# Attention, gated layer and rational layer on one core: when block 0 transposes, when the first pair is split, and in what order weights are streamed

## The chip, the cores and the metric

The kernel runs on one core of a Trainium2 chip. The metric is the device time of one execution in microseconds (us). A core has TensorE (PE in the profile, its weight loads PEld), VectorE (DVE), ScalarE (ACT), GpSimd (POOL) and SyncE (SP), which here issues nearly all DMA transfers. Each engine works off its own instructions in the order in which the program emits them and waits on semaphores for the others.

## The reference

All numbers are float32. There are 8 batches with 8 heads, 576 positions and head size 64; keys and values are averaged over 8 positions, so 72 of them remain.

```
k_p, v_p = mean over 8 positions of k, v
attn     = softmax(q @ k_p^T / 8) @ v_p             # -> x: 4608 tokens x 512
x        = (silu(x @ w_gate) * (x @ w_val)) @ w_out # 512 -> 1536 -> 512
h        = x @ w_in                                 # 512 -> 2048
out      = (a0 + a1 h + a2 h^2 + a3 h^3) / (1 + |b0||h| + |b1| h^2 + 1e-6) @ w_out2
```

## The kernel before, in words

The 4608 tokens are cut into nine blocks of 512. Each large product is made of three fp32r matmuls of 128x512 per tile: high times high, low times high and high times low part. `split` makes the parts: ACT copies a tile into fp32r (L97), DVE (L94) or POOL (L101) subtracts that from the source.

**Block 0** (L784 to L821) runs the gated layer plainly in 12 steps f = 0 to 11. A step emits for TensorE: the gate product gp (12 matmuls), the value product vp (12), and the output product acc of step f - 1 (12, `out_mm`). In each step `first.step(6)` runs three times; it carries the conversion of the weights one stage on (words and rounding on ACT, shifts, selects and low parts on DVE, an addition on POOL). Between these stands the attention of blocks 1 and 2, the first pair, in units of 128 or 64 rows. `attention_slots` puts the pieces of unit n into named places of the steps, and `place` emits them: scores (PE, tile sc) at the end of step n in place "C"; in step n + 1 `soft1` on DVE in place "0" (maximum L380 and subtraction L383, once for each of two score banks), the exponential on ACT in "A" (L393), and sums, division (POOL, L408) and copies in "B2"; in step n + 2 the transposes `t_` (PE, tile t) and, when a group of one or two units is complete, the products with the values `v_` (PE, tile pv). ACT moves the transposes out (L440, L441), DVE takes a low part (`evac_low`, L445), and ACT copies pv into xraw (L470). At a change of batch `v_` also calls `build_vs` (POOL L322, L330, then ACT L336). Units 0 to 8 have 64, 128, 128, 128, 64, 128, 128, 128, 128 rows; the groups are units 0; 1 and 2; 3 and 4; 5; 6 and 7; 8.

Scores, transposes and value products of block 0 take their PSUM banks from one pool of two:

```python
    ps_at = ctx.enter_context(tc.tile_pool(name="ps_at", bufs=2, space=PSUM))
    def bank(name, i=None):
        pool, tag = (ps_at, "at") if i is None else ...
```

One unit's scores take both banks, so do its transposes, and a group's value products take both as two halves (two head pairs in each).

**Pairs** (L886 to L962): the eight other blocks go in four pairs p through a seven-product scheme over 2x2 parts (n = 12 p + f, 48 steps). In a step TensorE has seven products of six matmuls: s1 t1, s2 t2, a22 t4 of step n - 1, a12 b21, s4 b22, a11 b11 of step n + 1, s3 t3. `token_sums` makes t1 to t4 by subtraction (L737), `token_part` splits tokens, `sum_weights` and `sum_splits` make s1 to s4 in the first pair, `sum_store` stores them, and `stream` loads them back for the other three pairs. In the same steps `second` (class `Halves`) converts the weights of the last layer: `begin` stores the finished half (L204), loads raw halves (L199) and starts conversion; of the buffers that it uses at first there are three. Then `hidden` outputs go to DRAM (L855) and q, k and v of the next blocks are loaded (L276). All these transfers stand in SP's one queue, in program order. The output product follows (L1022 to L1087; PSUM tiles ya, yb, yc), and then the rational layer (L1128 on).

Of the kernel before, what the change touches and what calls it, by code (L numbers as in the profile page):

```python
# [10 lines left out]
F32 = mybir.dt.float32  # L11
# [3 lines left out]
ALU = mybir.AluOpType  # L15
# [4 lines left out]
P = 128  # L20
B, H, S, D = 8, 8, 576, 64
# [43 lines left out]
def attention_gated_rational(  # L65
# [13 lines left out]
    def wslot(name, shape=(P, 2, 512), dt=F32R):  # L79
        return wp.tile(list(shape), dt, tag="w", name=name)  # L80

    def f32(ap):
        return ap.bitcast(F32)
# [402 lines left out]
    def attention_slots(js, start, helped=False, heads=False):  # L486


        def put(slot, place, fn):
            plan.setdefault((slot, place), []).append(fn)  # L490

        groups = [g for j in js for g in units(j)]
        owner = [j for j in js for g in units(j)]
        box = {}
        fl = [(g, i) for g in range(len(groups)) for i in range(len(groups[g]))]

        def do_xraw(j):
            if (j - PLAIN) % 2:
                live["w"] += 2
                st["xraw", j] = [wslot(f"xraw{j}_{i}", (P, 2, BLK), F32) for i in range(2)]  # L500
            else:
                t = keep.tile([P, KT, BLK], F32, tag="xraw", name=f"xraw{j}")
                st["xraw", j] = [t[:, 0:2, :], t[:, 2:4, :]]
        for n, (g, i) in enumerate(fl):
            u = groups[g][i]
            slot = start + n
            put(slot - 1, "B2", lambda u=u: box.__setitem__(("q", u), qload(u)))
            put(slot, "C", lambda u=u: box.__setitem__(("s", u), scores(u, box.pop(("q", u)), False, helped, heads)))
            put(slot + 1, "A0" if slot + 1 >= PLAIN * NF1 else "0", lambda u=u: box["s", u][0]())
            put(slot + 1, "0" if heads else "A", lambda u=u: box["s", u][1]())  # L510
            put(slot + 1, "B" if slot + 1 >= PLAIN * NF1 else "B2", lambda u=u: [fn() for fn in box.pop(("s", u))[2:]])

            def t_(u=u, g=g, i=i, at_bank=0 if slot + 2 >= PLAIN * NF1 else None):
                if i == 0:
                    box["pt", g] = new_pt(f"{js[0]}_{g}")
                for fn in transposes(u, box["pt", g], i * P, at_bank):
                    fn()
            put(slot + 2, "A", t_)
            if i + 1 == len(groups[g]):
                def v_(g=g):  # L520
                    j = owner[g]
                    if ("xraw", j) not in st:
                        do_xraw(j)
                    values(groups[g], box.pop(("pt", g)), st["xraw", j])
                    if g + 1 < len(groups) and groups[g + 1][0][0] != groups[g][0][0]:
                        build_vs(groups[g + 1][0][0])
                put(slot + 2, "B", v_)


    jobs = prep_jobs(0, early=True)  # L530
# [102 lines left out]
    def sum_weights(f):  # L633

        if f >= NF1:
            return
        rg, rv = sums_w[f] = [ldp.tile([P, 2, QUART], F32, tag="ld", name=f"r{x}{f}") for x in "gv"]
        for r, w in zip((rg, rv), (W1[f"g{f}"], W1[f"v{f}"])):
            nc.vector.tensor_tensor(r.rearrange("p h c -> p (h c)"), f32(w[:, 0, :]), f32(w[:, 1, :]), op=ALU.add)
        (a11, a12), (a21, a22) = ([r[:, h] for h in range(2)] for r in (rg, rv))  # L640
        nc.gpsimd.tensor_tensor(a22, a21, a22, op=ALU.add)
        nc.gpsimd.tensor_tensor(a21, a11, a21, op=ALU.subtract)
        nc.gpsimd.tensor_tensor(a11, a22, a11, op=ALU.subtract)
        nc.gpsimd.tensor_tensor(a12, a12, a11, op=ALU.subtract)

    def sum_splits(f):
        if f >= NF1:
            return
        rg, rv = sums_w.pop(f)
        w = [wslot(f"ws{f}_{i}") for i in range(2)]  # L650
        for i, r in enumerate((rv, rg)):
            split(w[i][:, 0, :], w[i][:, 1, :], r.rearrange("p h c -> p (h c)"))
        g_w, v_w = W1.pop(f"g{f}"), W1.pop(f"v{f}")
        streamed[f] = {
            "a11": (g_w, 0), "a12": (g_w, 1), "s3": (w[0], 0), "s1": (w[0], 1),
            "s2": (w[1], 0), "s4": (w[1], 1), "a22": (v_w, 1),
        }

    def sum_store(f):
        if f >= NF1:  # L660
            return
        x = streamed[f]
        for i, key in enumerate(("s1", "s2")):
            nc.sync.dma_start(s_d[f][i], f32(x[key][0]))
        if f < RESIDENT:
            nc.sync.dma_start(w_d[f], f32(x["a11"][0]))
            nc.sync.dma_start(v_d[f][:, :, QUART:], f32(x["a22"][0][:, :, QUART:]))
# [56 lines left out]
    def place(stage, f, p_):  # L724
        for fn in plan.pop((stage * NF1 + f, p_), []):
            fn()


    sums_x, parts_x = {}, {}

    def token_sums(p, eng):
        (b11, b21), (b12, b22) = (st.pop(("xraw", j)) for j in PAIRS[p])
        t1, t2, t3, t4 = (wslot(f"t{p}_{i}", (P, 2, BLK), F32) for i in range(4))

        def sub(out, x, y, eng=eng):
            for i in range(2):
                eng.tensor_tensor(out[:, i, :], x[:, i, :], y[:, i, :], op=ALU.subtract)  # L737
        sub(t1, b12, b11)
        sub(t2, b22, t1)
        sub(t3, b22, b12, nc.gpsimd)  # L740
        sub(t4, b21, t2, nc.gpsimd)
        sums_x[p] = {"b11": b11, "b21": b21, "b22": b22, "t1": t1, "t2": t2, "t3": t3, "t4": t4}
        parts_x[p] = {}

    FIRST_HOMES = {"b22": (0, 1), "t4": (2, 3)}

# [6 lines left out]
        for i in range(2):  # L753
            split(tiles[i][:, 0, :], tiles[i][:, 1, :], src[:, i, :])

    def stream(n):
        if NF1 <= n < len(PAIRS) * NF1:
            f = n % NF1
            w = [wslot(f"sw{n}_{i}") for i in range(4)]
            for t, src in zip(w, (s_d[f][0], w_d[f], s_d[f][1])):  # L760
                nc.sync.dma_start(f32(t), src)
            nc.sync.dma_start(f32(w[3][:, :, :QUART]), v_d[f][:, :, QUART:])
            streamed[n] = {
                "a11": (w[1], 0), "a12": (w[1], 1), "s3": (w[0], 0), "s1": (w[0], 1),
                "s2": (w[2], 0), "s4": (w[2], 1), "a22": (w[3], 0),
            }

    def part_product(acc, n, weights, tokens, first):
        w, c = streamed[n][weights]
# [7 lines left out]
    def out_mm(f):  # L777
        ht, w = h_t.pop(f), W1.pop(f"o{f}")
        for i in range(KT):
            mm3(acc[i], [(w, slice(i * P, (i + 1) * P), ht, full)], first=f == 0, last=f == NF1 - 1)  # L780
        live["w"] -= 1

    place(0, -1, "B2")
    for f in range(NF1):  # L784
# [30 lines left out]
        if f:  # L815
            out_mm(f - 1)
        place(0, f, "C")
        if f == NF1 - 2:
            sum_weights(0)
        if f == NF1 - 1:  # L820
            token_sums(0, nc.vector)  # L821
    first.finish()
    second.load()
    token_part(0, "b11")
    token_part(0, "t1")
    out_mm(NF1 - 1)
    ys = [wslot(f"ys_{i}", (P, 2, BLK), F32) for i in range(2)]
    for i in range(KT):
        nc.scalar.activation(ys[i // 2][:, i % 2, :], acc[i], AF.Copy)
# [49 lines left out]

        return 2 if n % 2 and n > NF1 + 2 else int(n > 0)  # L880

    sum_store(0)
    sum_weights(1)
    begin_chain(0)
    token_part(0, "t2")
    for n in range(full_n):  # L886
        p, f = divmod(n, NF1)
        stage = PLAIN + p
# [14 lines left out]
            second.paired = True  # L903
        second.begin(turns(n), turns(n + 1))
        part_product(bank_a[n], n, "s2", "t2", False)
        nc.vector.tensor_tensor(c, cq[n][:, 0, :], bank_a[n], op=ALU.add)  # L906
        if f == 0:
            if n == 0:
                token_part(p, "b21")
            token_part(p, "b22")  # L910
        place(stage, f, "A0")
        place(stage, f, "A")
# [4 lines left out]
            token_part(p + 1, "t2")  # L917
        second.middle()
        sum_splits(n + 1)
        stream(n + 2)  # L920
        b = bank_b.pop(n)
        part_product(b, n, "a12", "b21", False)
        if f == 0:
            token_part(p, "t3")
        hq[n] = wslot(f"hq{n}", (P, 2, BLK), F32)
# [7 lines left out]
        if n > 0:  # L933
            keep_hidden(n - 1)
        second.end()
        sum_store(n + 1)
        reload(n + 4)
        sum_weights(n + 2)
        if 0 < p < 3:
# [4 lines left out]
                (out_store if i else out_parts)(3 * p - 4 + r)  # L944
        place(stage, f, "B2")
        part_product(bank_a[n], n, "s3", "t3", False)
        nc.vector.tensor_tensor(cq[n][:, 1, :], cq[n][:, 0, :], bank_a[n], op=ALU.add)  # L947
        if f == 0:
            token_part(p, "t4")
# [3 lines left out]
        if p + 1 == len(PAIRS):  # L953
            if f == NF1 // 2 + 1:
                out_weights("a11")
                for k in range(5):
                    left_load(0, k)
            if f == NF1 - 2:
                left_load(0, 5)
                out_weights("s1")  # L960
            if f == NF1 - 1:
                out_weights("s2")  # L962
    NK = NF1 // 2
    TOKENS = ("b11", "t1", "t2", "b21", "t3", "b22", "t4")
# [56 lines left out]
    nc.scalar.preload_act_table_set("natural_log_exp_and_others")  # L1021
    for p, (j1, j2) in enumerate(PAIRS):  # L1022
        final = p + 1 == len(PAIRS)
        pool, tag = ((ps_gv, "gv"), (ps_at, "at"))[p % 2]
        ba = [pool.tile([P, BLK], F32, tag=tag, name=f"ya{p}_{q}") for q in range(2)]
        bb, bc = {}, {}
        box = {}
# [206 lines left out]
```

## Time and profile before

| what | us |
|---|---|
| three runs | 1772.21, 1769.96, 1768.76; median 1769.96 |
| profiled execution | 1774.04, of which the span shown is 1772.2 |
| PE busy | 1720.2 (97%), weight loads 1408.5 (79%) |
| DVE busy | 1425.7 (80%) |
| ACT busy | 1161.4 (66%) |
| POOL busy | 326.1 (18%) |
| mean granted TensorE clock | 0.993 of 2.4 GHz |

Busy time is the sum of an engine's instructions over the span. Block 0 lies between 36 and 182 us, the four pairs up to 755 us, the output product up to 985 us and the rational layer behind it.

### The profile page before, as it was taken

What the parts mean: (1) busy time and instruction counts of PE and PEld (TensorE: products, weight loads), DVE (VectorE), ACT (ScalarE), POOL (GpSimd) and SP (SyncE); (2) the same over time, 40 slices, a digit from 0 to 9 for tenths busy, and PEclk for the clock granted to TensorE, in tenths of its full rate; (3) what the DMA queues carried; (4) which work ended last, traced back from release to release, by engine and by line L of the source; (5) the groups of instructions that cost most, each with busy time, mean ns of one, the idle gap of its engine ahead of it and who ended that gap; (6) DMA issues with size and microseconds to landing.
All of it is one profiled execution on the core that took longest, in us unless ns stands there. A gap on an engine that the chain in (4) does not pass through costs nothing.

```text
span 1772.2 us, 23731 instructions
## 1 busy us (share of the span) xinstructions
PE 1720.2 (97%) x8104; PEld 1408.5 (79%) x8104; DVE 1425.7 (80%) x2325; ACT 1161.4 (66%) x2044; POOL 326.1 (18%) x412
## 2 busy tenths in 40 slices
PE   6898899999999999999999999999999999999999
PEld 5677677778878878778888788888888888888887
DVE  7998987777677664387778799989898989898987
ACT  5897766467577654455554677776777777777775
POOL 3455554534634431200000000000000000000000
PEclk9999999999999999999999999999999999999999
DMA  7775587899999899995517500000000000000000
GB/s 279 266 275 218 214 309 260 288 342 356 373 323 333 330 324 334 359 397 214 190 60 261 202 20 29 24 25 24 24 24 25 24 25 24 25 24 25 0 25 24
DMA packets 131736, 305.72 MB, mean 173 GB/s; under 512 B 12960, under 2 KB 53024, under 8 KB 130592
## 3 DMA queue, kind: packets, MB, share of 16 engines
q1 hardware_dynamic: 130752, 303.61, 47.4%
q8 instruction: 64, 1.05, 0.2%
q10 hardware_dynamic: 864, 0.60, 0.1%
q14 instruction: 56, 0.46, 0.1%
HBM read 207.16 MB, written 96.99 MB: 172 GB/s over the span
## 4 chain that ended last, share of the span: by engine, by line
PE 79%; DVE 8%; DMA 5%; ACT 3%; POOL 2%; issue 2%; SPq 1%; POOLq 0%; DVEq 0%; ACTq 0%
PE h L260 22%; PE acco L260 22%; PE ca L260 11%; PE ya L1077 6%; PE cc L260 6%; PE yc L1077 3%; PE cb L260 2%; PE yb L1077 2%; PE sc L372 1%; PE pv L461 1%; DMA q<-in_q 1%; POOL t L737 1%; DMA sw<-wd 1%; PE t L433 1%; DVE kr L291 1%
## 5 line engine op out<-in xcount | busy, mean ns | idle before, releaser
L260 PE MATMUL h<-z,wi 128*128 128x512 f32 x1728 | 414.7, 389 | 2.2 <-ACT yq L1046 2.2
L260 PE MATMUL acco<-wo,gt 128*128 128x512 f32 x1728 | 414.6, 389 | 0.0
L260 PEld LDWEIGHTS h<-z,wi 128*128 128x128 f32 x1728 | 324.2, 188 | 69.8 <-ACT yq L1046 2.6
L260 PEld LDWEIGHTS acco<-wo,gt 128*128 128x128 f32 x1728 | 324.4, 188 | 67.4
L1143 ACT ACTIVATE sq<-h 128x512 f32<-128x512 f32 x144 | 85.8, 596 | 176.0 <-PE h L260 176.0
L1150 DVE SCALAR_TENSOR_TENSOR w<-sq,neg,w 128x512 f32<-128x512 f32 x144 | 107.9, 750 | 43.8 <-ACT w L1144 43.7
L1164 ACT ACTIVATE gt<-g 128x512 fp32r<-128x512 f32 x144 | 90.9, 631 | 32.8 <-DVE g L1160 32.8
L1160 DVE SCALAR_TENSOR_TENSOR g<-t,neg,e 128x512 f32<-128x512 f32 x144 | 108.3, 752 | 5.1
L1156 DVE SCALAR_TENSOR_TENSOR t<-t,neg,h 128x512 f32<-128x512 f32 x144 | 107.7, 748 | 5.1
L1147 ACT ACTIVATE t<-h,neg 128x512 f32<-128x512 f32 x144 | 111.7, 776 | 0.0
L1157 DVE SCALAR_TENSOR_TENSOR e<-w,ln 128x512 f32<-128x512 f32 x144 | 98.6, 685 | 13.5 <-ACT ln L1154 13.5
L1154 ACT ACTIVATE ln<-ln,lnb 128x512 f32<-128x512 f32 x144 | 104.3, 724 | 4.7
L1144 ACT ACTIVATE w<-h,cab 128x512 f32<-128x512 f32 x144 | 98.6, 685 | 8.2 <-DVE e L1157 8.1
L1158 DVE SCALAR_TENSOR_TENSOR e<-e,ln 128x512 f32<-128x512 f32 x144 | 99.7, 692 | 5.0
L906 DVE TENSOR_TENSOR cc<-cq,ca 128x512 f32<-128x512 f32 x48 | 33.3, 693 | 84.0 <-PE ca L260 84.0
L1165 DVE TENSOR_TENSOR gt<-g,gt 128x512 fp32r<-128x512 f32 x144 | 99.0, 687 | 2.2 <-ACT gt L1164 0.8
L1155 DVE TENSOR_TENSOR t<-t,h 128x512 f32<-128x512 f32 x144 | 98.4, 683 | 0.0
L1153 ACT ACTIVATE ln<-w 128x512 f32<-128x512 f32 x144 | 91.5, 635 | 0.2 <-DVE w L1150 0.2
L901 ACT ACTIVATE cq<-cc 128x512 f32<-128x512 f32 x48 | 28.6, 596 | 86.6 <-PE cc L260 86.6
L947 DVE TENSOR_TENSOR cq<-cq,ca 128x512 f32<-128x512 f32 x48 | 32.5, 678 | 54.5 <-PE ca L260 54.5
L124 POOL TENSOR_TENSOR rawo<-rawo 128x256 uint32<-128x256 uint32 (+1 forms) x44 | 37.6, 855 | 147.8 <-DVE rawo L121 62.6
L408 POOL TENSOR_TENSOR p<-p,sm 128x576 f32<-128x576 f32 (+1 forms) x40 | 52.3, 1308 | 62.2 <-DVE sm L407 43.9
(276 smaller groups left out, 3455.1 us busy)
## 6 DMA issues: line engine op xcount, KB each, us to landing
sw<-sd SPq DMA_DIRECT2D x72, 512.0 KB, 6.8
h<-hq SPq DMA_DIRECT2D x48, 512.0 KB, 7.3
sw<-wd SPq DMA_DIRECT2D x36, 512.0 KB, 6.7
sd<-ws SPq DMA_DIRECT2D x24, 512.0 KB, 5.3
hl<-h SPq DMA_DIRECT2D x24, 512.0 KB, 6.5
hr<-h SPq DMA_DIRECT2D x24, 512.0 KB, 10.0
sw<-vd SPq DMA_DIRECT2D x36, 256.0 KB, 7.3
out<-ob SPq DMA_DIRECT2D x36, 256.0 KB, 2.2
```

Of the source, the lines that this page charges most:

```text
L260: nc.tensor.matmul(acc, st[:, lw, cols], mv[:, rw, mcols], start=first and i == 0, stop=last and i == n - 1, skip_group_check=seeded,)
L1077: nc.tensor.matmul(banks[q], w[:, lw, cols], t[:, rw, :], start=opened and k == 0 and m == 0, stop=k == NK - 1 and m == 2, skip_group_chec ...
L1144: nc.scalar.activation(w0, hps, AF.Abs, scale=cab[:, 4:5])
L1147: nc.scalar.activation(t, hps, AF.Identity, scale=neg[:, 3:4], bias=neg[:, 2:3])
L1150: nc.vector.scalar_tensor_tensor(w0, sq, neg[:, 5:6], w0, op0=ALU.mult, op1=ALU.add)
L1154: nc.scalar.activation(ln, ln, AF.Exp, scale=-1.0, bias=lnb)
L1155: nc.vector.tensor_tensor(t, t, hps, op=ALU.mult)
L1156: nc.vector.scalar_tensor_tensor(t, t, neg[:, 1:2], hps, op0=ALU.add, op1=ALU.mult)
L1157: nc.vector.scalar_tensor_tensor(e, w0, C1, ln, op0=ALU.add, op1=ALU.mult)
L1158: nc.vector.scalar_tensor_tensor(e, e, 2.0, ln, op0=ALU.subtract, op1=ALU.mult)
L1160: nc.vector.scalar_tensor_tensor(g, t, neg[:, 0:1], e, op0=ALU.add, op1=ALU.mult)
L1165: lambda gt=gt, g=g: nc.vector.tensor_tensor(gt[:, 1, :], g, f32(gt[:, 0, :]), op=ALU.subtract),
```

## The change

In block 0 the transposes move from place "A" (behind gp) to "B" (behind vp), and the value products from "B" to a new place "D" behind the scores. Of the first pair's sums, t1 and t2 and the split of b11 move to the end of step 10, the split of t2 ahead of the pairs; t3 and t4 move into step n = 0, on POOL. s1 and s2 now share one tile, s3 and s4 the other, by another order of the four POOL operations. `stream` loads single pieces, each behind the product that used that piece's predecessor. `sum_store` runs one step later, and the load of a raw half ahead of the pairs (`second.load()`) goes. Loads of `left_load` are spread over steps, and the two PSUM pools of ya swap.

```diff
-            put(slot + 2, "A", t_)
+            early = slot + 2 < PLAIN * NF1
+            put(slot + 2, "B" if early else "A", t_)
...
-                put(slot + 2, "B", v_)
+                put(slot + 2, "D" if early else "B", v_)
...
-        nc.gpsimd.tensor_tensor(a22, a21, a22, op=ALU.add)
-        nc.gpsimd.tensor_tensor(a21, a11, a21, op=ALU.subtract)
-        nc.gpsimd.tensor_tensor(a11, a22, a11, op=ALU.subtract)
-        nc.gpsimd.tensor_tensor(a12, a12, a11, op=ALU.subtract)
+        nc.gpsimd.tensor_tensor(a11, a11, a21, op=ALU.subtract)
+        nc.gpsimd.tensor_tensor(a21, a21, a22, op=ALU.add)
+        nc.gpsimd.tensor_tensor(a22, a22, a11, op=ALU.subtract)
+        nc.gpsimd.tensor_tensor(a12, a12, a22, op=ALU.subtract)
...
-    def stream(n):
+    def stream(n, *pieces):
         if NF1 <= n < len(PAIRS) * NF1:
...
+            for i in pieces:
+                w = wslot(f"sw{n}_{i}")
+                if i == 3:
+                    nc.sync.dma_start(f32(w[:, :, :QUART]), v_d[f][:, :, QUART:])
+                else:
+                    nc.sync.dma_start(f32(w), (w_d[f], s_d[f][0], s_d[f][1])[i])
...
         place(0, f, "C")
+        place(0, f, "D")
         if f == NF1 - 2:
             sum_weights(0)
-        if f == NF1 - 1:
-            token_sums(0, nc.vector)
+            token_sums(0, nc.vector, ("t1", "t2"))
+            token_part(0, "b11")
     first.finish()
-    second.load()
-    token_part(0, "b11")
     token_part(0, "t1")
     out_mm(NF1 - 1)
+    token_part(0, "t2")
...
-    sum_store(0)
     sum_weights(1)
     begin_chain(0)
-    token_part(0, "t2")
...
         part_product(bank_a[n], n, "s2", "t2", False)
+        stream(n + 2, 1)
...
                 token_part(p, "b21")
+                token_sums(0, nc.gpsimd, ("t3", "t4"))
             token_part(p, "b22")
...
         sum_splits(n + 1)
-        stream(n + 2)
+        stream(n + 1, 3)
         b = bank_b.pop(n)
         part_product(b, n, "a12", "b21", False)
+        stream(n + 2, 0)
...
-        sum_store(n + 1)
+        sum_store(n)
...
         part_product(bank_a[n], n, "s3", "t3", False)
+        stream(n + 2, 2)
...
-                for k in range(5):
-                    left_load(0, k)
+            if f >= NF1 // 2 + 2:
+                left_load(0, f - NF1 // 2 - 2)
...
-        pool, tag = ((ps_gv, "gv"), (ps_at, "at"))[p % 2]
+        pool, tag = ((ps_at, "at"), (ps_gv, "gv"))[p % 2]
```

## Rows read from the trace of the kernel before

**Rows 1.** Busy time by stretch; columns as named in the first line.
```profile
core 0: us, PE busy (x) PEld busy (x) DVE busy (x) ACT busy (x) POOL busy (x), PEclk, DMA share, GB/s
53.80:166.05 112.25, 103.78 (x564) 83.15 (x563) 104.56 (x196) 97.21 (x158) 53.23 (x60) 0.97 0.71 254
198.50:345.00 146.50, 137.27 (x700) 110.23 (x700) 117.41 (x201) 88.70 (x160) 84.08 (x102) 0.96 0.79 278
984.90:1772.20 787.30, 783.65 (x3456) 648.58 (x3456) 705.64 (x1041) 560.12 (x933) 0.00 (x0) 1.00 0.08 30
```

**Rows 2.** Waits of DVE, 50 to 166 us: total, times, longest.
```profile
DVE ptr L445 <- ACT ptr L440: 4.1, 9, 1.2
```

**Rows 3.** Timeline of PE, steps 4 and 5: start, length, instruction [idle before].
```profile
89.25 0.60 PE L461 MATMUL pv<-pt,vs 128*128 128x256 f32 x2
...
91.46 2.92 PE L260 MATMUL acc<-ht,wo 128*128 128x512 f32 x12
...
94.97 3.06 PE L260 MATMUL gp<-x,wg 128*128 128x512 f32 x12
97.86 0.60 PE L433 MATMUL t<-ident,p 128*128 128x128 f32 x4
```

**Rows 4.** Timeline of DVE in step 5.
```profile
96.63 0.45 DVE L383 TENSOR_TENSOR p<-sc,mx 64x288 f32<-64x288 f32 x1
...
97.47 0.45 DVE L383 TENSOR_TENSOR p<-sc,mx 64x288 f32<-64x288 f32 x1
...
100.04 0.42 DVE L445 TENSOR_TENSOR ptr<-t,ptr 32x256 fp32r<-32x256 f32 x1 [0.39 <-ACT ptr L440]
...
104.25 0.69 DVE L803 TENSOR_TENSOR hh<-hh,vp 128x512 f32<-128x512 f32 x1
```

**Rows 5.** Timeline of ACT, steps 4 and 5.
```profile
92.25 1.06 ACT L470 ACTIVATE xraw<-pv 128x512 f32<-128x512 f32 x2
...
96.04 0.67 ACT L155 ACTIVATE wo<-rawo 128x512 fp32r<-128x512 f32 x1 [0.51 <-POOL rawo L124]
...
97.85 1.28 ACT L794 ACT_TABLE_LOAD   x1
...
99.64 0.37 ACT L440 ACTIVATE ptr<-t 96x256 fp32r<-96x256 f32 x1
...
100.51 1.28 ACT L393 ACT_TABLE_LOAD   x1
...
102.40 0.67 ACT L155 ACTIVATE wg<-rawg 128x512 fp32r<-128x512 f32 x1
```

**Rows 6.** Timeline of POOL, then ACT, where `build_vs` runs.
```profile
127.13 1.49 POOL L322 TENSOR_TENSOR vs<-vp,vmask 128x512 f32<-128x512 f32 x1
...
129.40 0.42 ACT L336 ACTIVATE vr<-vt 96x256 fp32r<-96x256 f32 x1 [1.09 <-POOL vt L330]
```

**Rows 7.** Timeline of PE: what follows its longer waits.
```profile
59.78 0.69 PE L433 MATMUL t<-ident,p 64*128 64x64 f32 x4 [2.84 <-POOL p L408]
...
60.67 5.40 PE L260 MATMUL vp<-x,wv 128*128 128x512 f32 x12
...
249.99 1.12 PE L372 MATMUL sc<-kr,q 64*128 64x72 f32 x16 [1.11 <-DMA q<-in_q]
...
267.31 1.98 PE L372 MATMUL sc<-kr,q 64*128 64x72 f32 x16 [4.34 <-DMA q<-in_q]
269.22 2.93 PE L260 MATMUL cc<-x0t,ws 128*128 128x512 f32 x6
```

**Rows 8.** Timeline of PE at the start of the pairs.
```profile
184.18 0.50 PE L260 MATMUL ca<-x0b,wg 128*128 128x512 f32 x1 [0.50 <-DVE x0b L94]
...
188.34 0.49 PE L260 MATMUL ca<-x0t,ws 128*128 128x512 f32 x1 [0.65 <-DVE x0t L94]
```

**Rows 9.** Waits of SP's queue, 178 to 345 us.
```profile
SPq L199 <- DMA i_parts<-rawi: 33.1, 6, 6.7
```

**Rows 10.** Timeline of PE late in pair 4, and where the rational layer starts.
```profile
729.73 1.63 PE L260 MATMUL ca<-x3b,sw 128*128 128x512 f32 x6 [2.25 <-DMA sw<-wd]
...
984.91 11.17 PE L260 MATMUL h<-z,wi 128*128 128x512 f32 x48 [2.16 <-ACT yq L1046]
```

More of the change, by code (lines that the diff above doesn't have):

```diff
@@ L654, in sum_splits @@
         streamed[f] = {
-            "a11": (g_w, 0), "a12": (g_w, 1), "s3": (w[0], 0), "s1": (w[0], 1),
-            "s2": (w[1], 0), "s4": (w[1], 1), "a22": (v_w, 1),
+            "a11": (g_w, 0), "a12": (g_w, 1), "s1": (w[0], 0), "s2": (w[0], 1),
+            "s3": (w[1], 0), "s4": (w[1], 1), "a22": (v_w, 1),
         }
@@ L662, in sum_store @@
         x = streamed[f]
-        for i, key in enumerate(("s1", "s2")):
+        for i, key in enumerate(("s1", "s3")):
             nc.sync.dma_start(s_d[f][i], f32(x[key][0]))
@@ L726, in place, with token_sums @@
             fn()
[L729 to L735, printed above, removed]
-            for i in range(2):
[L737 to L743, printed above, removed]
+    sums_x, parts_x, raws_x = {}, {}, {}
+    def token_sums(p, eng, keys=("t1", "t2", "t3", "t4")):
+        if p not in sums_x:
+            (b11, b21), (b12, b22) = (st.pop(("xraw", j)) for j in PAIRS[p])
+            sums_x[p] = {"b11": b11, "b21": b21, "b12": b12, "b22": b22}
+            raws_x[p] = dict(sums_x[p])
+            parts_x[p] = {}
+        r = raws_x[p]
+        for key in keys:
+            x, y = {"t1": ("b12", "b11"), "t2": ("b22", "t1"), "t3": ("b22", "b12"), "t4": ("b21", "t2")}[key]
+            t = r[key] = sums_x[p][key] = wslot(f"{key}_{p}", (P, 2, BLK), F32)
+            for i in range(2):
+                eng.tensor_tensor(t[:, i, :], r[x][:, i, :], r[y][:, i, :], op=ALU.subtract)
+        if "t4" in keys:
+            sums_x[p].pop("b12")
     FIRST_HOMES = {"b22": (0, 1), "t4": (2, 3)}
@@ L754, in token_part @@
             split(tiles[i][:, 0, :], tiles[i][:, 1, :], src[:, i, :])
-    def stream(n):
+    def stream(n, *pieces):
         if NF1 <= n < len(PAIRS) * NF1:
[L758 to L766, printed above, removed]
+            f, held = n % NF1, streamed.setdefault(n, {})
+            for i in pieces:
[4 more added lines that the diff above has]
+                    nc.sync.dma_start(f32(w), (w_d[f], s_d[f][0], s_d[f][1])[i])
+                for c, key in enumerate((("a11", "a12"), ("s1", "s2"), ("s3", "s4"), ("a22",))[i]):
+                    held[key] = (w, c)
     def part_product(acc, n, weights, tokens, first):
@@ L955, in attention_gated_rational @@
                 out_weights("a11")
-                for k in range(5):
-                    left_load(0, k)
+            if f >= NF1 // 2 + 2:
+                left_load(0, f - NF1 // 2 - 2)
             if f == NF1 - 2:
-                left_load(0, 5)
                 out_weights("s1")
             if f == NF1 - 1:
+                left_load(0, 4)
+                left_load(0, 5)
                 out_weights("s2")
```

## The prediction, made before the changed kernel ran

> **What bounds the kernel now.** I read busy time by stretch first, then the waits, then the timelines of the places that change. The last stretch is TensorE's alone: 783.65 of 787.30 us busy at full clock [rows 1]. What the earlier stretches gain or lose therefore reaches the end undiminished. In the stretch of the first pairs, 198.5 to 345 us, PE is idle 146.50 - 137.27 = 9.2 us, and the granted clock is 0.96, which costs up to 4% of 146.5 = 5.9 us more [rows 1]. The reader is to see that block 0 differs. Over 53.8 to 166.05 us DVE is busy 104.56 of 112.25 us (93%), PE 103.78, ACT 97.21 [rows 1]. DVE is idle for 7.7 us there, 4.1 of them in nine waits for ACT's copy of the transposes [rows 2]. So three engines hand work round in a loop with little room, and a step of block 0 lasts as long as the longest way round.
>
> [...]
>
> **Part by part: transposes behind vp, value products behind the scores.** The old stalls of transposes on POOL go, the worst being 2.84 us with twelve matmuls behind it at half speed, 5.40 instead of 2.8 (48 take 11.17 us, so 0.233 each) [rows 7, 10]. But the value products now follow scores in TensorE's order, and both use the two banks of one pool. The scores fill both, and those are read only by `soft1`, at the head of DVE's next step. So pv of steps 2, 4, 6 and 7 (groups that end where scores are emitted in the same step) must wait for DVE's subtractions. Behind pv in PE's queue stand gp, vp and the next transposes; behind the xraw copy in ACT's queue stands the whole next step. In steps 9 and 10 no scores stand ahead.
>
> I walk it for step 4, on the times of before. The first subtraction ends at 96.63 + 0.45 = 97.1, the second at 97.9 [rows 4]. The four head pairs of pv take 91.46 - 89.25 = 2.2 us, each half 1.1 [rows 3]. So pv runs 97.2 to 98.3 and on to 99.3, where before gp had begun at 94.97 [rows 3]. ACT copies the second half out (1.06 / 2 = 0.53) until about 99.9. Then its queue holds: three copies 97.85 - 96.04 = 1.81, table load and Silu 99.64 - 97.85 = 1.79, table load and exponential 102.40 - 100.51 = 1.89, three more copies 1.81 and the copy of the transposes 0.37, together 7.67 [rows 5]. It ends at 107.5. PE's way (gp and vp 2.8 each, transposes 0.6) would end at 105.5, so ACT is last. DVE takes its low part (0.42) and begins hh at 107.9 to 108.0; before it began at 104.25, behind a wait of 0.39 [rows 4]. Step 4 thus costs 3.7 us. In step 6 the group has 192 columns, half a pv is 0.8, and the cost 3.4. In steps 2 and 7 the groups have 64 and 128 columns (half a pv by proportion 0.6 or less, so 3.2), but `build_vs` follows: ACT's copy ends at 129.40 + 0.42 = 129.8, 2.7 after POOL began at 127.13 [rows 6]; that is about 2.2 more than the xraw copies, so 5.4 each. The sum is 3.7 + 3.4 + 5.4 + 5.4 = +17.9.
>
> Against it, DVE's waits of 4.1 us go where no such pv precedes; four of about 0.39 are in the steps just compared, which leaves -2.5 [rows 2, 4]. The clock: PE now idles from the end of the scores (94.97) to 97.2, or longer, as acc and scores come earlier without pv ahead, so 2.2 to 4.4 us, four times. After 2.84 the row shows half speed for twelve matmuls (2.6 lost), after 2.16 none [rows 7, 10]. On the path each costs 0 to 2.6; ACT is last by 1.6 - 2.0, so I take 1.0 each, and take off the 2.6 lost today: +1.4. Block 0: 17.9 - 2.5 + 1.4 = **+16.8**, with bounds of -7.7 (all of DVE's idle time gone) and +28 (17.9 and four full losses of 2.6).
>
> The Trainium skill has a rule against this order (Perfetto Trace Analysis, Matmuls): independent groups should rotate through different banks, so that moving one out overlaps the next. No run here shows pv behind scores; by the rule the wait is exposed as walked, and without it the walk gives the second rival below.
>
> **First pair's splits.** Six DVE instructions (four subtractions, two low parts) move ahead; a 128x512 one with two inputs takes 0.69 [rows 4], so up to 4.1 us come before hh of step 11, and as much leaves the start of the pairs. There PE waited 0.50 for b11's and 0.65 for t2's low part [rows 8]; both are now long done: -1.15. The other waits there stay, since DVE's addition still stands ahead of b21. t3 and t4 are four POOL subtractions in step 0; the nearest POOL row is 1.49 [rows 6], so 6.0 us, with t3 done after 3.0. Three products of 1.4 lie in between, and t3's split stands behind `soft1` and an exponential anyway: 0, and +3 if POOL is late from its sums. The new order of the four sums makes the first tile one operation later, a step before use: 0. Bounds -5 to +4.
>
> **Conversion.** Today's load of a raw half waits for the store of the buffer's last content: 33.1 us in six waits, up to 6.7, for one of the two weights alone [rows 9]. With one half being stored, one converted and two loaded, four buffers are wanted and three there. Behind the blocked load stand the hidden store, the stores of sums, reloads and q. With one load less ahead three buffers suffice, the wait goes, and q is issued up to 6.7 us earlier. That frees PE's waits of 1.11 and 4.34, and the slow stretch behind the second: scores 1.98 instead of 1.12, six matmuls 2.93 instead of 1.4 [rows 7, 10]. Together 5.45 + 0.86 + 1.53 = **-7.8**, bounds 0 (another transfer holds SP) and -10. `sum_store` one step later only takes a wait off SP. A raw half then has one step instead of two to land: hidden, as a step lasts 9.8 us of matmuls alone (seven products of 1.4).
>
> **Streaming by pieces.** Same bytes. The piece with a11 and a12 is issued after a12 of n and used after s4 of n + 1, nine products of 1.4 = 12.6 us ahead at the least, before ten. Its one wait, 2.25 [rows 10], came behind a burst of eleven other loads, five of which are now spread: -2.25, bounds -3 and +5. **Pools of ya swapped.** The first product of the rational layer waited 2.16 for ACT to free its bank [rows 10]; two copies of 0.53 [rows 5] no longer stand ahead: -1.1, bounds 0 and -2.2.
>
> **Sum.** 16.8 - 1.15 - 7.8 - 2.25 - 1.1 = +4.5. The profiled execution took 1774.04 (span 1772.2 and 1.8 around it) and would take 1778.5. It lies 4.1 above the median of 1769.96, so the median becomes **1774.5**.
>
> **The rivals.** (a) *Forecast*, one loop over DVE, pv and ACT: 1774.5, its own range 1767 to 1783. For it: the order of program and the two banks. Against it: DVE may reach `soft1` sooner than in the walk.
>
> (b) *Faster: the bank wait is covered, only ACT's order counts.* If `soft1` is done when PE gets to pv, pv of step 4 ends at 97.2 and xraw at 97.7; ACT's 7.67 end at 105.4, and hh comes at 105.8, 1.6 late. Four times 1.6 and two `build_vs` of 2.2 are 10.8; less 2.5 and the old clock loss of 2.6, block 0 costs 5.7, and the sum is -6.6: 1763.4. It decides if DVE's wait-free loop runs 2 us ahead of PE. Against it: DVE is 93% busy.
>
> (c) *Faster: the old stalls go and nothing new comes*, up to DVE's 7.7: -7.7 - 12.3 = -20, 1750. It needs ACT's room too, and ACT has 15 us in 112 [rows 1].
>
> (d) *Slower still: the clock.* Each pv wait exceeds 2.84, and pv (1.1 of it) and gp behind it run at half speed on the path: 4 x (2.6 + 1.1) = 14.8 instead of 4.0, so 1785.
>
> (e) *The conversion doesn't free SP*: store and load of a half still meet, the q waits stay: 1774.5 + 7.8 = 1782.
>
> **How the numbers follow.** Chances: (a) 0.50, (b) 0.22, (c) 0.08, (d) 0.11, (e) 0.09. A measurement of this kernel tells about 0.2%, 3.5 us, from no change: 1766.4 to 1773.5. Case (a) lies above for 0.30, inside for 0.16 and below for 0.04; (b) is faster but for 0.03, (c) faster, (d) and (e) slower. Slower 0.50, same 0.19, faster 0.31. The range runs from 1757, below (b), to 1788, above (d); it leaves out (c) and the tails.
>
> **What would show it.** In the profile after: PE waits of 2 to 4 us at pv (L461) for DVE's L383, in four steps, and DVE waits of some 3 us at L445; the stretch from 53.8 to the first product of the pairs longer by about 16. No SP wait at L199 for parts stores, no PE wait for q near 250 and 267, none for sw late in pair 4. b11 and t2 without a wait. Wrong if block 0 is no longer than before: then the banks were free or DVE was ahead, and the time is that of (b) or (c).

## The result and the profile after

The changed kernel takes 1786.37 us (median of 6 runs, 1786.04 to 1787.14), the kernel before 1770.32 (6 runs, 1767.39 to 1772.21): ratio 1.0092, 95% interval 1.0079 to 1.0105, so 16 us slower. The forecast had +4.5: its direction was right and the time lies 1.6 us inside the upper end of its range, but the size was far too small.

In the profiled executions the difference is 12.4 us (span 1784.6 against 1772.2). The profiled run of before was 3.7 above its median, that of after (1786.42) was at its median; no trace shows where the other runs of before are shorter. The ledger below goes by the profiled pair. Its marks are read from PE's timeline: the first gp of steps 2 and 11, the first product of the pairs (ca), the first ya.

| us | before step 2 | step 2 to 11 | to the first ca | to the first ya | to the end |
|---|---|---|---|---|---|
| before | 53.80 | 112.25 | 16.32 | 570.30 | 1019.53 |
| after | 52.75 | 132.11 | 20.24 | 556.32 | 1023.18 |
| difference | -1.05 | +19.86 | +3.92 | -13.98 | +3.65 |
| forecast | 0 | +16.8 | 0 | -11.2 | -1.1 |

Busy time by stretch, after (the loop of block 0, all four pairs, the rational layer), and then the four pairs of before:

```profile
core 0: us, PE busy (x) PEld busy (x) DVE busy (x) ACT busy (x) POOL busy (x), PEclk, DMA share, GB/s
52.75:184.86 132.11, 111.09 (x565) 89.38 (x563) 104.28 (x194) 96.39 (x155) 54.43 (x60) 0.90 0.61 217
205.10:761.42 556.32, 547.37 (x2788) 443.15 (x2786) 381.82 (x689) 342.11 (x639) 245.21 (x319) 0.99 0.90 327
996.24:1784.60 788.36, 784.51 (x3456) 648.77 (x3456) 708.01 (x1044) 562.46 (x937) 0.00 (x0) 1.00 0.08 31
```

```profile
182.37:752.67 570.30, 551.54 (x2787) 445.20 (x2786) 386.75 (x697) 342.71 (x640) 243.53 (x317) 0.99 0.89 321
```

DVE and ACT do the same work in the loop as before (104.3 and 96.4 us) in 20 us more: the loss is waiting. PE's own 7.3 us more are its clock, 0.90 instead of 0.97. In the pairs PE is idle for 8.9 us instead of 18.8, which is most of the 14 us gained there; the rational layer takes 1 us more. PE's waits of the whole run begin:

```profile
PE pv L461 <- DVE p L383: 14.9, 4, 4.3
PE vp L260 <- DVE wv L94: 9.3, 5, 5.4
...
PE yc L1082 <- ACT h0t L97: 3.5, 1, 3.5
```

The first row is the wait that the forecast named: four times, up to 4.3 us. The other two that are shown it did not have. PE's timeline shows the four pv waits and the gate products behind them (start, length, [idle before]):

```profile
70.56 0.66 PE L461 MATMUL pv<-pt,vs 128*128 128x64 f32 x2 [3.54 <-DVE p L383]
...
73.69 4.60 PE L260 MATMUL gp<-x,wg 128*128 128x512 f32 x12
...
95.92 0.72 PE L372 MATMUL sc<-kr,q 64*64 64x72 f32 x16 [0.95 <-ACT pt L441]
100.93 1.19 PE L461 MATMUL pv<-pt,vs 128*128 128x256 f32 x2 [4.29 <-DVE p L383]
...
104.89 2.90 PE L260 MATMUL gp<-x,wg 128*128 128x512 f32 x12
...
130.49 0.98 PE L461 MATMUL pv<-pt,vs 128*128 128x192 f32 x2 [3.95 <-DVE p L383]
...
133.99 3.50 PE L260 MATMUL gp<-x,wg 128*128 128x512 f32 x12
...
147.82 0.46 PE L461 MATMUL pv<-pt,vs 128*128 128x128 f32 x2 [3.13 <-DVE p L383]
...
149.88 4.06 PE L260 MATMUL gp<-x,wg 128*128 128x512 f32 x12
```

DVE and then ACT around the wait of step 4 (at 100.93), for [rows 4, 5]:

```profile
100.33 0.45 DVE L383 TENSOR_TENSOR p<-sc,mx 64x288 f32<-64x288 f32 x1
...
101.18 0.45 DVE L383 TENSOR_TENSOR p<-sc,mx 64x288 f32<-64x288 f32 x1
...
106.27 0.69 DVE L94 SCALAR_TENSOR_TENSOR wo<-rawo,wo 128x512 fp32r<-128x512 f32 x1 [2.91 <-ACT wo L155]
...
113.20 0.42 DVE L445 TENSOR_TENSOR ptr<-t,ptr 32x256 fp32r<-32x256 f32 x1 [3.39 <-ACT ptr L440]
113.65 0.69 DVE L805 TENSOR_TENSOR hh<-hh,vp 128x512 f32<-128x512 f32 x1
```

```profile
103.44 0.60 ACT L470 ACTIVATE xraw<-pv 128x512 f32<-128x512 f32 x1 [4.54 <-PE pv L464]
105.09 0.60 ACT L470 ACTIVATE xraw<-pv 128x512 f32<-128x512 f32 x1 [1.06 <-PE pv L464]
105.59 0.65 ACT L155 ACTIVATE wo<-rawo 128x512 fp32r<-128x512 f32 x1
...
112.81 0.36 ACT L440 ACTIVATE ptr<-t 96x256 fp32r<-96x256 f32 x1
```

pv starts 0.15 after the first subtraction ends; ACT's queue behind the second copy lasts from 105.69 until the copy of the transposes ends at 113.17, 7.48 (walked: 7.67); DVE waits for it, takes its low part and begins hh at 113.65. Every link of the walk is there. What was not in it is the speed of pv: 100.93 to 104.89 is 3.96 us where 2.2 were taken from [rows 3]. The granted clock in these two stretches, after and before (PEclk, the third column from the end), is 0.56 and 1.00, so pv ran at little more than half speed:

```profile
100.93:104.89 3.96, 3.96 (x12) 3.37 (x13) 2.36 (x5) 0.60 (x1) 2.81 (x4) 0.56 0.52 187
```

```profile
89.25:91.46 2.21, 2.21 (x13) 1.99 (x12) 2.17 (x6) 2.20 (x4) 0.72 (x1) 1.00 0.74 292
```

Step 11, with the first pair's splits in front, on DVE and then on PE:

```profile
188.60 1.82 DVE L743 TENSOR_TENSOR t<-xraw,xraw 128x512 f32<-128x512 f32 x2
190.34 2.34 DVE L743 TENSOR_TENSOR t<-xraw,t 128x512 f32<-128x512 f32 x2
192.60 1.81 DVE L94 SCALAR_TENSOR_TENSOR x0b<-xraw,x0b 128x512 fp32r<-128x512 f32 x2
194.33 0.68 DVE L94 SCALAR_TENSOR_TENSOR wv<-rawv,wv 128x512 fp32r<-128x512 f32 x1
```

```profile
195.06 2.07 PE L260 MATMUL vp<-x,wv 128*128 128x512 f32 x4 [5.42 <-DVE wv L94]
196.93 4.33 PE L260 MATMUL acc<-ht,wo 128*128 128x512 f32 x12
```

The low part of the value weights (wv), which the last four products of vp need, stands behind 6 us of the pair's work; PE waits 5.42 and the output products behind it then run slow, 4.33 instead of 2.9 [rows 3].

What went away is visible too. Of SP's waits at L199 for stores [rows 9] only a 1.0 for another store is left in 200 to 345 us, the q waits [rows 7] and the sw wait [rows 10] are gone, and the first product h waits 0.34 instead of 2.16 [rows 10]. SP still stands, now 27.2 us in four waits of its hidden store for DVE, but PE waits for no q. New in the output product is PE's wait for what SP's right-hand loads bring; these start 7.6 us after the first ya, before 3.8 us (756.44 and 752.67):

```profile
SPq L199 <- DMA wd<-wg: 1.0, 1, 1.0
```

```profile
769.00 5.71 SPq L1019 DMA_DIRECT2D hr<-h  x6
```

```profile
773.91 9.83 PE L1082 MATMUL yc<-h0t,os 128*128 128x512 f32 x36 [3.48 <-ACT h0t L97]
...
996.24 1.02 PE L260 MATMUL h<-z,wi 128*128 128x512 f32 x2 [0.34 <-ACT z L97]
```

### The profile page after: what moved, and what is told of

Its sections match the earlier page's. It is cut to its first block, busy times and chain, and to the rows that moved or that the text cites. A ratio compares the mean times of both kernels' runs of the same rounds, so it can differ in the third digit from the quotient of the medians.

```text
span 1784.6 us, 23661 instructions
## 1 busy us (share of the span) xinstructions
PE 1725.3 (97%) x8104; PEld 1413.4 (79%) x8104; DVE 1425.8 (80%) x2325; ACT 1162.4 (65%) x2044; POOL 325.5 (18%) x412
## 3 DMA queue, kind: packets, MB, share of 16 engines
q8 instruction: 64, 1.05, 0.2%
## 4 chain that ended last, share of the span: by engine, by line
PE 81%; DVE 4%; DMA 2%; POOL 1%; ACT 1%; issue 1%; SPq 0%; POOLq 0%; DVEq 0%; ACTq 0%
PE h L260 22%; PE acco L260 22%; PE ca L260 12%; PE ya L1082 6%; PE cc L260 6%; PE yc L1082 4%; PE cb L260 3%; PE yb L1082 2%; PE sc L372 1%; PE pv L461 1%; POOL t L743 1%; PE t L433 1%; DMA yraw<-y 0%; DMA hl<-h 0%; PE acc L260 0%
## 5 line engine op out<-in xcount | busy, mean ns | idle before, releaser
L1159 ACT ACTIVATE ln<-ln,lnb 128x512 f32<-128x512 f32 x144 | 104.3, 724 | 4.7
L461 PE MATMUL pv<-pt,vs 128*128 128x256 f32 (+3 forms) x208 | 54.0, 368 | 17.6 <-DVE p L383 14.9
```

Source lines behind the costliest of these rows:

```text
L1159: nc.scalar.activation(ln, ln, AF.Exp, scale=-1.0, bias=lnb)
```

## The experiments

Each of the twelve is timed against the kernel before on the same chip (its medians there: 1772.12 for the first four, 1771.33 for the next four, 1770.24 for e9 to e11, 1771.19 for e12). Stages as in the ledger, from one profiled run each.

| | median us | ratio to before, 95% | step 2 to 11 | to ca | to ya | to end |
|---|---|---|---|---|---|---|
| e1 places back | 1766.16 | 0.9959 (0.9939 to 0.9978) | 111.03 | 18.75 | 557.00 | 1024.13 |
| e2 own banks | 1773.45 | 1.0003 (0.9994 to 1.0013) | 120.00 | 19.01 | 556.20 | 1024.71 |
| e3 splits back | 1785.29 | 1.0066 (1.0047 to 1.0086) | 132.31 | 16.23 | 558.04 | 1021.84 |
| e4 conversion alone | 1765.43 | 0.9954 (0.9939 to 0.9969) | 111.67 | 16.05 | 562.45 | 1020.78 |
| e5 left loads back | 1786.32 | 1.0087 (1.0072 to 1.0102) | 133.79 | 20.53 | 559.10 | 1017.66 |
| e6 three parts back | 1763.60 | 0.9956 (0.9939 to 0.9972) | 111.72 | 15.53 | 564.10 | 1018.28 |
| e7 transposes back | 1771.97 | 1.0003 (0.9994 to 1.0012) | 120.25 | 19.36 | 554.52 | 1020.98 |
| e8 streaming back | 1784.88 | 1.0083 (1.0068 to 1.0098) | 132.04 | 20.10 | 556.47 | 1021.99 |
| e9 values first | 1775.68 | 1.0033 (1.0020 to 1.0046) | 121.54 | 19.90 | 556.69 | 1023.79 |
| e10 left loads between | 1764.19 | 0.9968 (0.9956 to 0.9980) | 111.13 | 13.97 | 560.35 | 1023.40 |
| e11 three small edits | 1763.15 | 0.9958 (0.9944 to 0.9971) | 112.28 | 16.29 | 557.40 | 1022.46 |
| e12 values early | 1774.66 | 1.0016 (1.0006 to 1.0027) | 124.89 | 13.34 | 560.17 | 1022.69 |

**e1.** In the changed kernel both pieces go back to their old places.

```diff
-            put(slot + 2, "B" if early else "A", t_)
+            put(slot + 2, "A", t_)
...
-                put(slot + 2, "D" if early else "B", v_)
+                put(slot + 2, "B", v_)
```

> The changed kernel with one part undone: block 0's transposes and value products stand where they stood before (behind gp, behind vp); all else is as changed. Theory (value products behind the scores wait for a bank, and the loop through DVE and ACT gets longer): steps 2 to 10 of block 0, which went from 112.2 to 132.1 us, come back to about 112; 1786.4 - 19.9 = 1766.5, some 4 below the kernel before, and no wait of pv for L383. Rival (block 0 got longer because the first pair's subtractions and splits now share DVE with it): the wait of vp in step 11 and most of the 20 us stay, 1780 or more.

1766.16 us, block 0 at 111.03: the two places cost 20 us and with them the whole loss; the rest of the change is a gain. The loop, the clock with it:

```profile
53.49:164.52 111.03, 101.48 (x564) 81.03 (x563) 103.78 (x196) 97.05 (x159) 52.95 (x60) 1.00 0.72 257
```

**e2.** The places stay, but block 0's value products use the two banks of gate and value.

```diff
-                both = bank(f"pv{b}_{o}_{pr}", None if parts is None else pr // 2 * 2)
+                both = bank(f"pv{b}_{o}_{pr}", pv_bank if parts is None else pr // 2 * 2)
```

(`pv_bank` is 0 in block 0, otherwise None.)

> The changed kernel, with the value products of block 0 in the two banks of gp and vp instead of the two of the scores; their order stays. It tells the bank wait from the order of ACT's queue. Theory: the four waits of pv for DVE's second subtraction, 14.9 us in all, go, and 9 to 14 us of the 20 come back: 1772 to 1777; the rest (the copy of the transposes later in ACT's queue) stays. Rival (the bank wait only shows slack that DVE and ACT need anyway): the waits move to other instructions of PE, and the time stays within 3 us of 1786.

1773.45 us lies in the expected range. All four pv waits are gone, and 12.1 us of block 0. So the shared banks are what the forecast said they are. 9.0 us against e1 stay. PE's waits in the loop:

```profile
PE sc L372 <- ACT pt L441: 8.8, 3, 4.2
PE vp L260 <- DVE wv L94: 2.4, 2, 2.1
```

ACT's waits in the loop, and ACT in step 2 and 3:

```profile
ACT vr L336 <- POOL vt L330: 9.2, 2, 4.7
```

```profile
73.52 0.42 ACT L336 ACTIVATE vr<-vt 96x256 fp32r<-96x256 f32 x1 [4.73 <-POOL vt L330]
...
81.35 0.59 ACT L441 ACTIVATE pt<-t 128x512 f32<-128x512 f32 x1
```

ACT stands still for `build_vs` at the head of its step, 4.73 and 4.49 us (before: 2.9 in both together), the copy of the transposes comes later, and scores wait 4.17 and 4.00 for it, in steps 3 and 8. Only 2.3 of the 4.73 are POOL's two instructions of `build_vs` (71.25 to 73.49); until then POOL works on what stands ahead of them in its queue. With shared banks this ACT wait is only 2.5 us in all, since POOL does that other work during the pv wait. So 12 and 9 are not two separate bills of the change; part of the second shows when the first is paid.

**e7, e9 and e12** try the rest of block 0. e7 is e2 with the transposes at "A" again (the first pair of lines of e1).

> The changed kernel with block 0's transposes at their old place, ahead of vp, and the value products behind the scores but in the two banks of gate and value instead of those of the scores. Theory: of the 19.9 us that block 0 lost, 12.1 were the shared banks (measured with the value products in their own banks: 120.0 us), and the 7.8 that stayed are the transposes' place: ACT copies pt later, and scores wait for it (8.8 us in three waits). So block 0 comes back to 112 to 113 us, and the time is 1766. Rival: the 7.8 come from the value products' own late place, which delays the xraw copies and the value weights' low part: block 0 stays at 119 to 121 us and the time near 1773.

Block 0 stays at 120.25 and the time is 1771.97: my theory fell, with banks of their own for the value products the transposes' place costs nothing that shows. (It was not put back alone in the shared banks.) Their old stall only returns, "PE t L433 <- POOL p L408" now 9.6 us in four waits, and ACT waits 6.3 for vt.

e9 puts value products ahead of the scores, in the shared banks:

```diff
-        place(0, f, "C")
         place(0, f, "D")
+        place(0, f, "C")
```

> The changed kernel with the value products of block 0 still behind the output products, but ahead of the scores instead of behind them; all else as changed, the two banks shared. Theory: what the shared banks cost (12 us) is that scores nobody reads before DVE's next step lie in both when the value products come. Ahead of the scores the banks are free, the waits of value products for DVE's subtractions (14.9 us in four) go, and what stays is ACT's part, the copies of the value products at the head of its next step (about 8 us, as with banks of their own): block 0 119 to 122 us, the time 1772 to 1774. Rival: two tenants of one pool stall in either order, now the scores behind the copies of the value products: block 0 128 to 132 us, the time 1782 to 1786.

The pv waits for DVE go; block 0 is 121.54, as expected, and the time is 1.7 above what I gave. Block 0 takes 10.6 us less when the tenant that nobody is about to read comes second. PE's waits in the loop, and ACT's:

```profile
PE sc L372 <- ACT xraw L470: 5.5, 4, 1.9
PE sc L372 <- ACT pt L441: 2.5, 1, 2.5
```

```profile
ACT vr L336 <- POOL vt L330: 8.9, 2, 4.6
```

e12 is e7 with the value products in "B2", ahead of the output products.

```diff
-                put(slot + 2, "D" if early else "B", v_)
+                put(slot + 2, "B2" if early else "B", v_)
```

> As the variant with the transposes back at their old place and value products in banks of their own, but the value products between the low part of the hidden tile and the output products, so that ACT can copy them out within their own step. Theory: the 8 us that stay with banks of their own come from the copies of the value products, which wait until the output products and scores are done and then stand at the head of ACT's next step, ahead of the table load and Silu. Issued before the output products they are done in the step: block 0 112 to 114 us, the time 1765 to 1767. Rival: the cost is in the two extra tenants of the banks of gate and value, which the next gate product wants: block 0 stays at 118 to 122 us, the time at 1771 to 1774.

Neither number came: 124.89 to step 11, but 13.34 behind it, 138.2 together against 139.0 (e2) and 139.6 (e7). ACT's wait for vt falls to 3.2 us, and in its place value products wait for their new banks, which vp holds until DVE multiplies:

```profile
PE pv L461 <- DVE hh L805: 10.4, 6, 2.4
```

This edit brings in a cost of its own, so it doesn't separate the late copies from the rest. What makes the last 9 us is therefore shown only in part. From one hh to the next on DVE, e2 loses 7.3 us against before over steps 3 to 10, of which the two steps with `build_vs` (3 and 8) hold 4.9; in e7 they hold 5.1 of 7.8, in e9 4.6 of 10.1, with 4.3 in step 7, where no `build_vs` stands. No run removed `build_vs` alone, and the rest stays open.

**e3.** The first pair's t1, t2 and b11 go back behind step 11, t2's split behind the first product.

```diff
         if f == NF1 - 2:
             sum_weights(0)
+        if f == NF1 - 1:
             token_sums(0, nc.vector, ("t1", "t2"))
-            token_part(0, "b11")
     first.finish()
+    token_part(0, "b11")
     token_part(0, "t1")
     out_mm(NF1 - 1)
-    token_part(0, "t2")
...
     begin_chain(0)
+    token_part(0, "t2")
```

> The changed kernel with t1, t2 and the split of b11 back at the end of step 11 and t2's split back behind the first product of the pairs. Theory (six DVE instructions put ahead of step 11 hold up the low part of its weights, for which vp waits 5.42 us, with half clock behind): that wait goes, b11 and t2 cost about 1.15 again, and the time is 1786.4 - 4.4 = 1782, between 1780 and 1783. Rival (step 11 waits for POOL's and ACT's sums anyway, the wait only moves to the output product): within 1.5 us of 1786.

Step 11 to the first product is 4.0 shorter, the 5.42 wait gone; the old one comes back (PE, first row below), and 1.7 are lost behind it. Expected were 1780 to 1783; the median of four runs that differ by up to 3.3 us is 1785.29, 1.1 below after's, while the ratio to before is 0.0026 lower (4.6 us). So the theory holds in the trace, and the times do not settle how much of it is paid.

```profile
197.26 4.71 PE L260 MATMUL acc<-ht,wo 128*128 128x512 f32 x12 [2.20 <-ACT ht L807]
```

```profile
197.85 1.28 DVE L743 TENSOR_TENSOR t<-xraw,xraw 128x512 f32<-128x512 f32 x2
199.06 1.28 DVE L743 TENSOR_TENSOR t<-xraw,t 128x512 f32<-128x512 f32 x2
```

**e4.** In the kernel before, only the early load goes.

```diff
     first.finish()
-    second.load()
     token_part(0, "b11")
```

> The kernel before with one edit: the raw half that was loaded ahead of the pairs is not, so conversion loads one turn ahead instead of two. Theory (SP's load waited for a store of the same buffer, and q behind it): no wait of SP at L199 for parts in the first pair, no waits of PE for q near 250 and 267 us, 1770.3 - 8 = 1762, between 1760 and 1764. Rival (SP is then held by the next instruction in its queue, and the 13.5 us gained in the pairs come from streaming by pieces and later stores of the sums): within 2 us of 1770.

Ratio 0.9954, 8.1 us, or 6.7 by the two medians. 1765.43 lies just above the expected 1760 to 1764, which were reckoned from 1770.3; before took 1772.12 there. Between the first ca and the first ya it takes 7.85 less, forecast 7.8. The q waits are gone; the sw wait (2.1) and that of h (2.7) stay.

**e8.** In the changed kernel the four loads of a step stand together again: `stream(n + 2, 1, 0, 2, 3)` where `stream(n + 1, 3)` was, the other three calls out.

> The changed kernel with the four streamed weights of a step loaded at one place again, two steps ahead, as before. From the first product of the pairs to the first ya product the change saved 14.0 us, of which the earlier conversion alone gave 7.85 and the first pair's splits 1.7. Theory: the spread loads gave the other 4.4 us (2.2 of it the wait for the streamed weights in the last pair): the stretch becomes 558.6 to 560.7 us instead of 556.3, the time 1788.5 to 1791. Rival: the spread gives nothing beyond noise, the rest came with the conversion and the pools: 556 to 557 us, 1786 to 1787.

The rival holds: 556.47 to ya, 1784.88. Streaming by pieces gives nothing, and the sw wait stays away without it.

**e5.** The left loads as before.

```diff
-            if f >= NF1 // 2 + 2:
-                left_load(0, f - NF1 // 2 - 2)
+                for k in range(5):
+                    left_load(0, k)
```

(and the sixth at f = 10 instead of the last two at f = 11.)

> The changed kernel with the loads of the left halves issued as before (five in a burst, the sixth three steps later). Theory: spread out, the last of them stand ahead of the rational layer's right-hand loads in SP's queue, so that these start 7.6 us after the first ya product instead of 3.8, and PE waits 3.48 us for h0t at yc. With the burst the wait goes: from the first ya product to the end 1020 us instead of 1023.2, about 3 us less, 1783.4 against 1786.4. First rival: the yc wait comes from the swapped pools, so it stays at 3.4 and the time is 1786. Second rival: the burst brings back the wait for the streamed weights in the last pair (2.1 to 2.25 us), so that only 1 us is gained: 1785.5.

The yc wait goes, 5.5 us behind the first ya; the sw wait returns with 2.8 ahead of it. So this burst made the wait that the forecast gave to streaming. The time is the same, 1786.32: block 0 was 1.7 longer in the profiled run, and by the medians the trade gives nothing.

**e6, e10 and e11** combine. e6: e1, e3 and e5 in one kernel. e10: e6 with left loads two, one, one, two in four steps. e11: the kernel before with e4's edit, e10's loads and the swapped pools.

> The changed kernel with three parts as before: the places of block 0's transposes and value products, the first pair's splits, and the burst of left loads; of the change the earlier conversion, the streaming by pieces and the swapped pools stay. Theory: the costs are those of three places one behind another and add up. 52.75 to the first gp of the loop, 111.5 to the last, 16.2 to the first product of the pairs, 558 to the first ya product and 1020 behind it are a span of 1758.5, so 1760.3 us, 10 us under the kernel before. Rival: what one place gives is taken back by a wait at the next, and the time is that of the variant with the places alone put back, 1764 to 1766.

> The variant with three parts as before (places, first pair's splits, left loads), but the six left loads neither in one burst nor up to the last step: two at the old place of the burst, one in each of the next two steps, two in the step after. Theory: the burst causes the wait for streamed weights in the last pair (3.0 us in that variant), and loads up to the last step hold back the right-hand loads (the wait of 3.5 us at yc); between the two both go: 3.0 less than 1763.6, so 1760.6 us. Rival: any six loads there crowd one or the other, and 1763 to 1764 stays.

> The kernel before with three small edits: the conversion one turn ahead, the pools of the rational layer swapped, and the left loads two, one, one, two in four steps instead of five in a burst and one. Theory: 1765.4 with the conversion alone, less 2.1 for streamed weights in the last pair, less 1.9 to 2.5 for the swapped pools: 1761 us, as fast as anything with more of the change in it. Rival: streaming by pieces or the moved sums do carry a part, and it stays 2 us or more above the other variant of this call.

Expected 1760.3, 1760.6 and 1761; measured 1763.60, 1764.19 and 1763.15. All three missed by 2 to 4 us: the gains of single places did not add up. All lie with e1 and e4 at 0.9954 to 0.9968, intervals overlapping. One edit, the conversion, carries the whole gain that can be measured. PE's waits from the pairs to the last product, in e6 and in e10:

```profile
PE ca L260 <- DMA sw<-wd: 3.0, 1, 3.0
```

```profile
PE yc L1083 <- ACT h0t L97: 3.6, 1, 3.6
```

Each kernel has one of the two: sw 2.25 (before), 2.8 (e5), 3.0 (e6), with yc at most 0.4; or yc 3.5 (after), 2.8 (e8), 3.6 (e10), 2.7 (e11), with no sw. In e10 the right-hand loads start 6.9 us after the first ya, in e6 3.9. SP issues them 24.2 and 22.2 us after a blocked load (L199, 7.3 and 5.4 us). I read this as one chain of transfers that PE meets earlier or later; a run that shortens the chain wasn't made.

## Why the prediction was right in direction and too small

The range held partly by luck. Its top, 1788, was set by rival (d), whose 1785 is also the nearest of the rivals' times; but of (d)'s mechanism only the slow pv came on the path, and the rest of the miss has other causes, below.

- **Block 0, +16.8: +19.9.** The bank wait and ACT's queue behind it are shown by e1, e2 and e9. What failed is the step that carried the cost of step 4 over to steps 2, 6 and 7 by the size of pv. Behind the pv of steps 2, 4, 6 and 7, the round from one hh to the next took 18.4, 17.8, 17.3 and 17.4 us after, nearly the same four times, but 13.9, 12.1, 10.3 and 14.3 before: +4.5, +5.7, +7.0 and +3.1, together 20.3. The forecast had 6.4, 4.7, 4.4 and 6.4 with 1.0 of clock in each, together 21.9; its errors of up to 3.3 us cancel, so that block 0 came near is in part luck too. The round behind step 6 was the shortest before (hh below), and the walk did not look at it; `build_vs` adds about 1.7 us (a wait of 1.2 and a copy of 0.42) and not 2.2, in rounds that were already the longest. The clock was mis-sized as well: pv itself ran slow on the path (1.8 in step 4, as much in step 6). The rounds behind step 6, on DVE, before and after:

```profile
115.72 0.69 DVE L803 TENSOR_TENSOR hh<-hh,vp 128x512 f32<-128x512 f32 x1
...
126.03 0.69 DVE L803 TENSOR_TENSOR hh<-hh,vp 128x512 f32<-128x512 f32 x1
```

```profile
125.41 0.69 DVE L805 TENSOR_TENSOR hh<-hh,vp 128x512 f32<-128x512 f32 x1
...
142.29 0.42 DVE L445 TENSOR_TENSOR ptr<-t,ptr 32x256 fp32r<-32x256 f32 x1 [5.22 <-ACT ptr L440]
142.74 0.69 DVE L805 TENSOR_TENSOR hh<-hh,vp 128x512 f32<-128x512 f32 x1
```

- **The rest of block 0.** The -5.1 (2.5 of DVE's short waits, 2.6 of the old clock loss) never came. In the rounds without pv only one of DVE's waits at L445 is left, 0.28, but these four rounds got 0.3 longer, not shorter. The old stall of step 2 is gone, but hh of step 2 comes 12.73 us after the first gp of its step, before 12.66: hh had not waited for it. Rival (b) lost by its condition, DVE isn't ahead of PE. Of rival (d) the slow gp behind pv came too (4.60, 2.90, 3.50 and 4.06 us), but off the path: in the loop ACT waits for no gp.
- **First pair's splits, -1.15: +3.9 ahead of the pairs, some of it given back.** The failing step is "up to 4.1 us come before hh of step 11, and as much leaves the start of the pairs". The moved work took 6.0 and stood ahead of wv's low part, for which PE waits; I had looked at hh only. Two of the stalls named are gone, as forecast.
- **Conversion, -7.8: -7.85 (e4 alone).** Right, mechanism and size.
- **Streaming, -2.25: the wait went, but by the spread left loads (e5, e8).** They had no price of their own in the sum. Spread, they gave 2.8 ahead of ya and cost 5.5 behind it. With the conversion's 7.85 and the 1.7 of e3 the 2.8 make 12.35 of the 13.98 gained between ca and ya; the other 1.6 no run explains.
- **Pools swapped, -1.1: about -1.9** (e5's last stage against before's, 1017.66 and 1019.53).
- **From trace to median.** I took 4.1 off because the profiled run of before lay above its median. After's run did not, which alone is 4.0 of the 11.9 that were missed (1786.37 - 1774.5). The rest by stages: -1.05 before the loop, 3.1 in block 0, 3.9 in step 11, -2.8 in the pairs, 4.75 behind ya, together 7.9.

## What to carry to other kernels

Ask of a moved product who reads what already lies in its banks, and when: behind scores that are read only in the next step, value products cost 10.6 us more than ahead of the scores, in the same banks. When work is moved ahead on a busy engine, price everything that is queued behind its new place, not only the consumer that you had in mind. A wait that is removed by coming earlier is worth only what the next deadline leaves; here the waits for sw and for yc took turns in seven kernels.

## What the runs showed of the hardware

- The same four DVE subtractions took 1.29 + 1.29 us before and 1.28 + 1.28 in e3, where POOL stands idle beside nearly all of them, but 1.82 + 2.34 in after, where POOL adds (1.05 to 1.12 each) at that time. The Trainium skill (GPSIMD Engine Reference, Specifications) says that POOL's way to the memory is shared with VectorE and contends with its instructions of two inputs; the rows agree.
- What a wait of PE costs in clock varies from run to run at the same place. Behind one wait of 2.65 to 2.69 us for DVE's cc (at 339.5 us in before, 352.4 in after, 354.1 in e5) three groups of six matmuls took 2.93, 2.77 and 1.98 in before; 2.00, 2.76 and 1.64 in after; 1.66, 1.52 and 1.52 in e5. The granted clock over these stretches was 0.57 (339.54 to 346.80), 0.72 (352.43 to 358.43) and 1.00 (354.06 to 358.44). Sums of stages in single profiles scatter accordingly: the loop of block 0, the same program in after, e8 and e5, took 132.11, 132.04 and 133.79.
